# Efficient attention followed by a SwiGLU block: the order of the early loads, the last store and the written-out order of steps

## The chip, the cores and the metric

The kernel runs on one core of one Trainium2 chip. The metric is the device time of one execution in microseconds. A core has TensorE (PE, matmul; PEld is its weight load), VectorE (DVE), ScalarE (ACT), GpSimd (POOL) and SyncE (SP), which here only issues DMAs. Each engine works through its own queue in program order and waits on semaphores for the others.

## The reference

Eight batches of eight heads, 576 positions, head size 64. The attention has no score matrix: q is normalized by a softmax over the head dimension, k by a softmax over positions, and a 64 x 64 product of k and v is applied to q. A gated feed-forward block follows.

```python
q_s = softmax(q, axis=-1)                    # 8 x 8 x 576 x 64
k_s = softmax(k, axis=2)
kv = np.einsum('bhsd,bhse->bhde', k_s, v)
attn = np.einsum('bhsd,bhde->bhse', q_s, kv)
x = attn.transpose(0, 2, 1, 3).reshape(4608, 512)
g = x @ w_gate                               # 512 x 1536
out = (g * sigmoid(g) * (x @ w_val)) @ w_out # 1536 x 512, fp32 out
```

## The kernel before

**Attention, by batch b and group G.** A batch is loaded as six DMAs, q, k and v for each of two groups of four heads, 576 KB each, issued from SP (`load`, L89). The raw tiles of q and k have three buffers, those of v two. `exp` (eq, ek; L127) runs on ACT. `norm_sum` (ns; L143, L147) sums q's exponentials and takes reciprocals on DVE; `norm_mul` (nm with a DMA transpose, nd without; L152) scales them. `cast_v` (cv, L118 or L116) rounds v to bf16. `kv_pair` (kv) or `kv_kn` (kk) forms and normalizes the 64 x 64 products on PE (L192); `x_pair` (xx) or `x` (xz) multiplies q with them and writes the feed-forward input into the ring `xt`. In batches 0 and 1 q is transposed on PE (`tr`, L168), later by a DMA transpose issued from SP (`tr_dma`, L180).

**Feed-forward.** The tokens are taken in chunks: `chunk(-1)` holds batch 0's 576 tokens, chunk 0 the next 448, chunks 1 to 8 the rest, 512 tokens each; chunk 8 only finishes the output product. In chunk -1 the 12 blocks of 128 hidden columns are plain matmuls: `I` m computes the gate product and its Silu on ACT (L321), `J` m the value product and the multiplication on DVE (L324), into the ring `hr`. In later chunks some blocks are plain (`G`, `U`: L435), and the others are pairs `a` to `g` that use a seven-product (Strassen) scheme (L384); their weight sums `gt` come from `g_sum` (Q, T; L336) and their token sums `xs` from `x_sum` (X, Y). In the output product, `O` j s is half s of a plain 128-token unit (L473), of which chunk -1 has four; the letters `A` to `F` and `H` are the seven products of a 512-token `Quad` (L526), with sums `wt` (W) and `hs` (S) made on DVE. Results are copied to o_sb, of which there are five buffers, and stored with two DMAs of 64 rows for each 128 rows (`store`, L462).

**Weights.** `w_slice` (L104) and `wo_slice` (L112) load fp32 weights from HBM and round them to fp16 on the way; they are issued from GpSimd. wg and wv come in slices of 256, 256, 512 and 512 columns, wg and wv in turn, then w_out in three slices of four blocks (`wo`). The first waits for v(0,0) to land, and q of batch 1 waits for the first slice of w_out:

```python
load(1, 0, "q", q, after=w_dma[-3])
load(1, 1, "q", q)
for G in range(NG):
    load(1, G, "k", k)
    load(1, G, "v", v)
load_group(2, 0)
```

**Order.** The program order on every engine is the order of emission, and that is written out by hand: `PLAN_B` (chunk -1, with the attention of batch 1 and part of batch 2), `PLAN_0` (chunk 0), `PLAN` (chunks 1 to 5, with the attention of batch ci + 2 inside), `PLAN_N` (6 and 7), `PLAN_E` (8). A star moves a step to another engine: for Q, nd and xx from GpSimd or DVE as coded in `op`, for the products' copies from ACT to DVE, for e and g the multiplication from GpSimd to DVE, for H the copies from DVE to ACT. PSUM has eight banks in one pool; an I or J step takes two. ACT's exp and Silu need different tables, and each change between them puts an ACT_TABLE_LOAD into ACT's queue.

Of the kernel before, what the change touches and what calls it, by code (L numbers as in the profile page):

```python
# [16 lines left out]
def kernel(  # L17
# [19 lines left out]
    nc = tc.nc  # L37

    B, H, S, D = q.shape
# [58 lines left out]
    def w_slice(dst, src, c0, n):  # L98
        ap = bass.AP(
            tensor=src.tensor,  # L100
            offset=src[0, c0].offset,
            ap=[[d_ff, 128], [128 * d_ff, KT], [1, n]],
        )
        return nc.gpsimd.dma_start(out=dst[:, :, c0:c0 + n], in_=ap)  # L104

    def wo_slice(m0, n):
        ap = bass.AP(
            tensor=moe_w_out.tensor,
            offset=moe_w_out[m0 * 128, 0].offset,
            ap=[[d_model, 128], [128 * d_model, n], [1, d_model]],  # L110
        )
        return nc.gpsimd.dma_start(out=wo[:, m0:m0 + n, :], in_=ap)  # L112
# [187 lines left out]
    class First:  # L300
# [14 lines left out]

        def run(self, step, alt=False):
            if step == "I":
                self.sg = []
                for p_, (c, n) in zip(self.mm(wg, "g_ps"), self.parts):
                    self.sg.append(ff.tile([128, 512], FP32, tag="sg", name="sg"))  # L320
                    nc.scalar.activation(out=self.sg[-1][:, 0:n], in_=p_[:, 0:n], func=AF.Silu)  # L321
            else:
                for p_, sg, (c, n) in zip(self.mm(wv, "u_ps"), self.sg, self.parts):
                    nc.vector.tensor_mul(hr[:, self.m, c:c + n], sg[:, 0:n], p_[:, 0:n])  # L324

    def g_cols(w, kh, c0, c1):
        return w[:, 2 * kh:2 * kh + 2, :].rearrange("p k (j c) -> p k j c", j=2)[:, :, :, c0:c1]
# [22 lines left out]
            eng.tensor_sub(s[3], a12, s[1])  # L350

    def sg_tile():
        return ff.tile([128, 512], FP32, tag="sg", name="sg")

    class Pair:
        def __init__(self, c0, h, n, tsum, tc0):
# [147 lines left out]
    class Quad:  # L504
        def __init__(self, Q, kks, own=False):
            self.Q, self.r, self.kks = Q, (512 * Q) % RING, kks
            pool = (lambda n: ld.tile([128, 512], FP32, tag=n, name="os")) if own else None
            self.s_tile = (
                (lambda n: pool("q" if n == "s1" else "k")) if own
                else lambda n: sn.tile([128, 512], FP32, tag=n, name=n)  # L510
            )
            self.o_sb = [[None, None], [None, None]]

        def ot(self, t, p):
            if self.o_sb[t][p] is None:
# [42 lines left out]
        def run(self, step, alt=False):  # L558
            ceng = nc.vector if alt else nc.scalar
            two_f = lambda n: [f_tile(n) for _ in range(2)]  # L560
            if step == "A":
                self.x, self.s1 = two_f("ox"), self.two("s1")
                self.prod(self.x, self.raw_h(0, 0), self.raw_w(0, 0), True)
                self.copies(self.s1, self.x, ceng)
            elif step == "B":
                y = two_f("oy")
                self.prod(y, self.raw_h(1, 0), self.raw_w(1, 0), True)
                self.add(0, 0, y, self.s1)
            elif step == "C":
                self.w, self.s5 = two_f("ow"), self.two("s5")  # L570
                self.prod(self.w, self.sum_h(0), self.sum_w(0), True)
                self.copies(self.s5, self.w, ceng)
            elif step == "D":
                self.s2 = self.two("s2")
                self.prod(self.x, self.sum_h(1), self.sum_w(1), False)
                self.copies(self.s2, self.x, ceng)
            elif step == "F":
                self.prod(self.x, self.sum_h(2), self.sum_w(2), False)
                self.add(1, 1, self.x, self.s5)
            elif step == "E":  # L580
                self.prod(self.w, self.sum_h(3), self.raw_w(1, 1), False)
                self.add(0, 1, self.w, self.s2)
                self.store(0)
            elif step == "H":
                self.prod(self.x, self.raw_h(1, 1), self.sum_w(3), False)
                for p in range(2):
                    copy(
                        nc.scalar if alt else nc.vector,
                        self.ot(1, p)[:, 0:HN], self.x[p][:, 0:HN],
                    )  # L590
                    store(4 * self.Q + 2 + p, self.ot(1, p))

    make_identity(nc, ident)
    with tc.manual_schedule():
# [20 lines left out]
        cast_v(0, 0, nc.scalar)  # L615

        w_dma = []
        for c0, n in ((0, 256), (256, 256), (512, 512), (1024, 512)):
            w_dma.append(w_slice(wg, moe_w_gate, c0, n))
            w_dma.append(w_slice(wv, moe_w_val, c0, n))  # L620
        tc.add_manual_dep(w_dma[0].ins, dmas["v", 0, 0].ins.name, SYNC, reason="order of loads")
        for m0 in (0, 4, 8):
            w_dma.append(wo_slice(m0, 4))

        warm_up(WARM[0])
        for G in range(NG):
# [17 lines left out]
        x(0, 1, A)  # L644
        x(0, 1, Z)

        load(1, 0, "q", q, after=w_dma[-3])
        load(1, 1, "q", q)
        for G in range(NG):
            load(1, G, "k", k)  # L650
            load(1, G, "v", v)
        load_group(2, 0)

        n_ch = n_tok // 512 - 1

        def op(t, ci, c0, h, parts):
# [5 lines left out]
            if nm in ATT:  # L662
# [3 lines left out]
                if nm == "eq":  # L666
                    exp(b, G, "q")
                elif nm == "ek":
                    exp(b, G, "k")
                elif nm == "si":  # L670
                    nc.scalar.activation(out=warm, in_=warm, func=AF.Silu)
                elif nm == "cv":
                    cast_v(b, G, nc.vector if alt else nc.gpsimd)
                elif nm == "ns":
                    norm_sum(b, G)
                elif nm == "nm":
                    norm_mul(b, G, nc.vector if alt else nc.gpsimd)
                    tr_dma(b, G)
                elif nm == "lo":
                    if ci < 0:  # L680
                        load_group(b, 1)
                    else:
                        load_group(b + 1, 0)
                        load_group(b + 1, 1)
                elif nm == "kv":
                    kv_pair(b)
                elif nm == "xx":
                    x_pair(b, nc.scalar if alt else nc.vector)
                elif nm == "nd":
                    norm_mul(b, G, nc.gpsimd if alt else nc.vector)  # L690
                elif nm == "tr":
                    tr(1, G, BANKS[int(t[3])], nc.vector)
                elif nm == "kk":
# [48 lines left out]
        ORDER = (0, 1, 2, 3, 4, 5)  # L742
        gt2 = [None] * 4
        PLAN_B = """
        I0 J0 I1 I2 J1 J2 I3 J3 I4 I5 J4 J5 I6 I7 J6 I8 Q0* J7 J8 I9 I10 Q2* Q1* J9 eq0:1
        Q3 J10 eq1:1 I11 ns0:1 ns1:1 J11 ek0:1 ek1:1 nd1:1 O01 nd0:1* cv0:1 O11 O02* tr00
        cv1:1 O12 tr10 tr11 kk0:1 eq0:2 cv0:2 load:2 tr01 O21 xz00 kk1:1 xz01* ns0:2 O22
        nm0:2 ek0:2 xz10* O31 cv1:2 xz11 eq1:2 O32 ek1:2
"""
        PLAN_0 = """  # L750
        a0 b0 ns1 load v0 Y0 G4 a1 Y2 Y1* kv U4 c0 d0 G10 f0 b1 c1 Y3 nm1 W0 g0 d1 v1 a2
        e0 f1 e1 b2 c2 g1 d2 W1 v2 U10 a3 f2 G5 b3 g2 v3 e2 c3 d3* xx* e3 U5 f3 W2 X0 X2
        X1 G11 U11 g3* X3 W3
"""
        PLAN = """
        S002 G4 S022 S102 a0 b0 G10 d0 c0 A v0 a1 S042 eq0 S122 S142 S302 B S342 f0 S242
        b1 ek0 U4 S322 D S222 ek1 e0 eq1 cv0 S202 C* v1 cv1 g0 ns0 F E d1 H* a2 ns1 c1 f1
        silu nm0 b2 c2 nm1 e1 g1 d2* v2 a3 U10 f2 e2 load kv b3 g2 c3 d3 G5 v3 e3* f3 xx*
        X0 G11 U5 X1 U11 g3* X3 X2
"""  # L760
        PLAN_N = """
        a0 b0 c0 d0 A v0 T0* f0 S002 a1 b1 g0 d1 c1 S022 S102 S222 v1 e0 a2 S202 f1 e1 b2
        S042 c2 g1 d2 v2 S122 B f2 a3 T1 b3 c3 S242 S142 g2 e2 d3 S322 D v3 a4 f3 T2 C g3
        T3 d4 b4 e3 c4 v4 f4 S302 F a5 g4 b5 S342 d5 v5 e4 c5* f5 E X0 X1 e5* X3 X2* g5*
        H*
"""
        PLAN_E = """
        S202 S042 S022 S002 A S142 S122 S102 B C S322 S302 S342 D S222 S242 E F H*
"""
        chunk(-1, 0, S, PLAN_B)  # L770
        chunk(0, S, 1024 - S, PLAN_0)
# [33 lines left out]
```

The softmax here doesn't subtract the row's maximum and nothing guards it: scores larger than these inputs give would overflow.

## Time and profile before

| | us |
|---|---|
| median of 6 runs (lowest to highest) | 303.02 (302.1 to 306.46) |
| the profiled execution, its own time | 302.34 |
| its span in the trace | 300.3 |
| PE busy | 289.7 |
| DVE, ACT, POOL busy | 232.2, 210.7, 136.6 |
| chunk -1: first I to the end of the O steps | 15.57 to 57.6 |
| mean granted TensorE clock | 0.992 |

All times in the text are microseconds from the start of the span unless said otherwise. A line of a timeline has start, length, engine, line, operation, out<-in, shapes and count; in square brackets stands how long the engine sat idle before it and what released it. A row of waits has the sum, the number and the longest. Landing is the time from the start of a DMA's issue to its completion.

### The profile page before, as it was taken

The numbers are of one execution on the slowest core, as the hardware profiler recorded it, in microseconds if no ns is written. First come the engines' busy times: TensorE is split into PE (matmuls) and PEld (weight loads), VectorE is DVE, ScalarE is ACT, GpSimd is POOL, SyncE is SP. The second block draws the span as 40 slices with busy tenths as digits, with TensorE's granted clock in tenths as the row PEclk, the third lists the DMA queues.
The fourth block names the chain that finished last, engine by engine and source line by source line (L and its number), as shares of the span: only waits on it lengthen the run. The fifth ranks groups of instructions, "written<-read, shape, count | busy, mean of one in ns | idle before, by whom it ended". The sixth has DMA issues, their size and how long they took to land.

```text
span 300.3 us, 6895 instructions
## 1 busy us (share of the span) xinstructions
PE 289.7 (96%) x2644; PEld 227.8 (76%) x2644; DVE 232.2 (77%) x497; ACT 210.7 (70%) x385; POOL 136.6 (45%) x108
## 2 busy tenths in 40 slices
PE   8999979979999999999999999999999999999993
PEld 6777735568688758875887588758886888888882
DVE  2943956678898787888788878877888898895981
ACT  5754377687798579857995899479948776667530
POOL 1940165358309900890089008900794455275500
PEclk9999997999999999999999999999999999999999
DMA  7999999999003991289228931992180000600066
GB/s 268 273 182 206 236 395 310 293 268 314 0 3 68 175 389 62 62 168 368 99 52 174 357 111 40 194 387 75 43 180 0 2 0 4 139 2 0 3 139 140
DMA packets 38863, 46.43 MB, mean 155 GB/s; under 512 B 16304, under 2 KB 21936, under 8 KB 38832
## 3 DMA queue, kind: packets, MB, share of 16 engines
q1 hardware_dynamic: 33024, 41.30, 48.1%
q0 software_dynamic: 5808, 4.72, 10.2%
q8 instruction: 20, 0.33, 0.4%
q14 instruction: 11, 0.09, 0.1%
HBM read 37.75 MB, written 9.44 MB: 157 GB/s over the span
## 4 chain that ended last, share of the span: by engine, by line
PE 74%; DMA 16%; POOL 3%; SPq 2%; issue 1%; ACT 1%; DVE 1%; POOLq 0%; ACTq 0%; DVEq 0%
PE sx L384 19%; PE ox L526 14%; PE sw L384 10%; PE ow L526 7%; PE u_ps L435 7%; PE g_ps L435 6%; DMA wo<-in_moe_w_out_dram 5%; DMA v<-in_v_dram 5%; PE sy L384 5%; PE oy L526 3%; DMA qtd<-qs 3%; DMA q<-in_q_dram 2%; PE kv L192 2%; POOL vb L118 1%; POOL wg L104 1%
## 5 line engine op out<-in xcount | busy, mean ns | idle before, releaser
L418 POOL TENSOR_TENSOR hr<-sg,s 128x512 bf16<-128x512 f32 (+1 forms) x29 | 37.9, 1306 | 75.0 <-DVE s L417 74.0
L384 PEld LDWEIGHTS <-gt 128*128 128x128 f16 x576 | 56.2, 98 | 10.5 <-issue 0.7
L426 POOL TENSOR_TENSOR hr<-sg,s 128x512 bf16<-128x512 f32 (+1 forms) x28 | 35.6, 1270 | 35.4 <-ACT sg L425 35.4
L384 PE MATMUL sx<-xs,gt 128*128 128x256 f16 (+1 forms) x288 | 42.8, 271 | 0.0
L116 ACT COPY s<-sx 128x512 f32<-128x512 f32 (+1 forms) x66 | 38.2, 579 | 5.0 <-PE sx L384 4.2
L526 PEld LDWEIGHTS <-hs 128*128 128x128 bf16 x384 | 37.6, 98 | 5.4
L417 DVE TENSOR_TENSOR s<-sw,s 128x512 f32<-128x512 f32 (+1 forms) x36 | 24.5, 681 | 16.8 <-PE sw L384 16.5
L425 ACT ACTIVATE sg<-sx 128x512 f32<-128x512 f32 (+1 forms) x36 | 21.2, 590 | 19.9 <-PE sx L384 12.9
L152 POOL TENSOR_TENSOR qs<-eq,rr 128x1152 bf16<-128x1152 bf16 x14 | 29.5, 2120 | 11.4 <-DVE rr L147 11.4
L384 PEld LDWEIGHTS <-wg 128*128 128x128 f16 x288 | 27.7, 98 | 5.2
L421 DVE TENSOR_TENSOR s<-sx,s 128x512 f32<-128x512 f32 (+1 forms) x36 | 24.4, 679 | 8.9 <-ACT s L116 4.7
L526 PEld LDWEIGHTS <-hr 128*128 128x128 bf16 x288 | 28.2, 98 | 3.3
L143 DVE TENSOR_REDUCE rs<-eq 128x18 f32<-128x1152 bf16 x16 | 21.4, 1338 | 9.7 <-ACT eq L127 9.7
L410 ACT ACTIVATE sg<-s 128x512 f32<-128x512 f32 (+1 forms) x36 | 22.6, 626 | 8.0 <-DVE s L408 7.9
L116 ACT COPY s<-sw 128x512 f32<-128x512 f32 (+1 forms) x34 | 19.8, 583 | 8.9 <-PE sw L384 3.8
L408 DVE TENSOR_TENSOR s<-sy,s 128x512 f32<-128x512 f32 (+1 forms) x36 | 24.3, 674 | 1.4 <-ACT s L116 0.7
L435 PE MATMUL g_ps<-xt,wg 128*128 128x512 f16 (+1 forms) x96 | 24.3, 375 | 0.0
L526 PE MATMUL ox<-wt,hs 128*128 128x256 f16 x192 | 23.6, 273 | 0.0
L435 PE MATMUL u_ps<-xt,wv 128*128 128x512 f16 (+1 forms) x96 | 23.4, 375 | 0.0
L384 PE MATMUL sy<-xt,wg 128*128 128x256 f16 (+1 forms) x144 | 21.4, 271 | 0.0
L384 PE MATMUL sw<-xs,wv 128*128 128x256 f16 (+1 forms) x144 | 21.4, 271 | 0.0
L384 PE MATMUL sx<-xt,gt 128*128 128x256 f16 (+1 forms) x144 | 21.4, 271 | 0.0
(99 smaller groups left out, 570.8 us busy)
## 6 DMA issues: line engine op xcount, KB each, us to landing
q<-in_q_dram SPq DMA_DIRECT2D x16, 576.0 KB, 6.7
k<-in_k_dram SPq DMA_DIRECT2D x16, 576.0 KB, 8.4
v<-in_v_dram SPq DMA_DIRECT2D x16, 576.0 KB, 8.8
out_dram<-o_sb SPq DMA_DIRECT2D x72, 128.0 KB, 2.4
wo<-in_moe_w_out_dram POOLq DMA_DIRECT2D x3, 512.0 KB, 18.2
wg<-in_moe_w_gate_dram POOLq DMA_DIRECT2D x2, 512.0 KB, 11.1
wv<-in_moe_w_val_dram POOLq DMA_DIRECT2D x2, 512.0 KB, 12.7
wg<-in_moe_w_gate_dram POOLq DMA_DIRECT2D x2, 256.0 KB, 5.7
```

The costliest lines, as they stand in the source:

```text
L116: nc.scalar.copy(out=out, in_=in_)
L143: nc.vector.reduce_sum(out=rs, in_=s["eq"].rearrange("p t h d -> p (t h) d"), axis=mybir.AxisListType.X)
L152: eng.tensor_mul(s["qs"].rearrange("p t (h d) -> p (t h) d", d=64), s["eq"].rearrange("p t h d -> p (t h) d"), s["rr"].to_broadcast([128, ...
L384: nc.tensor.matmul(out=bank[:, h * j:h * j + h], lhsT=wgt(kk, j), rhs=rhs[:, kk, 0:h], start=first and j == 0 and kk == 0, stop=kk == 1, s ...
L408: nc.vector.tensor_add(self.s1, self.y[:, 0:w], self.s1)
L410: nc.scalar.activation(out=self.sa[:, 0:w], in_=self.s1, func=AF.Silu)
L417: nc.vector.tensor_add(self.s2, self.w[:, 0:w], self.s2)
L418: meng.tensor_mul(self.out(0), self.halves(self.sa), self.halves(self.s2))
L421: nc.vector.tensor_add(self.s5, self.x[:, 0:w], self.s5)
L426: meng.tensor_mul(self.out(1), self.halves(sb), self.halves(self.s5))
L435: nc.tensor.matmul(out=ps[:, 0:self.n], lhsT=w[:, kk, 128 * self.m:128 * self.m + 128], rhs=xt[:, kk, self.r:self.r + self.n], start=(kk = ...
L526: nc.tensor.matmul(out=dst[p][:, 0:HN], lhsT=lhs(kk, p), rhs=rhs(kk), start=start and i == 0, stop=i == HM - 1, skip_group_check=True,)
```

## The change

- Weights: wv's first two slices become one of 512 columns, and both first slices of wg go ahead of it. `w_dma` then has wg 0, wg 256, wv 0, wg 512, wv 512, wg 1024, wv 1024, w_out 0, 4, 8, numbered from 0. The first slice of w_out waits on GpSimd for wg 1024 to land.
- Loads: q of batch 1 waits for wv 512. k and v of batch 1 wait for w_out 4, w_out 8 and one another; batch 2's loads wait each for an earlier load of the chain. The load of v(2,1) alone stays at the plan's `load`.
- The Silu results of an I step share one tile of 576 columns in place of two of 512; the buffers stay four.
- In the last Quad, the second half of each of H's stores is issued from ACT.
- All five plans have a new order, and some stars change: in `PLAN_B` Q0 and nd1 move to GpSimd; in `PLAN` a2's copy moves to DVE, C's copies to ACT and e3's multiplication to GpSimd; in `PLAN_E` D's copies move to DVE.

```diff
-                self.sg = []
-                for p_, (c, n) in zip(self.mm(wg, "g_ps"), self.parts):
-                    self.sg.append(ff.tile([128, 512], FP32, tag="sg", name="sg"))
-                    nc.scalar.activation(out=self.sg[-1][:, 0:n], in_=p_[:, 0:n], func=AF.Silu)
+                ps = self.mm(wg, "g_ps")
+                self.sg = ff.tile([128, S], FP32, tag="sg", name="sg")
+                for p_, (c, n) in zip(ps, self.parts):
+                    nc.scalar.activation(
+                        out=self.sg[:, c:c + n], in_=p_[:, 0:n], func=AF.Silu
+                    )
...
-                    store(4 * self.Q + 2 + p, self.ot(1, p))
+                    engs = (nc.sync, nc.scalar) if self.last else (nc.sync, nc.sync)
+                    store(4 * self.Q + 2 + p, self.ot(1, p), engs=engs)
...
-        for c0, n in ((0, 256), (256, 256), (512, 512), (1024, 512)):
-            w_dma.append(w_slice(wg, moe_w_gate, c0, n))
-            w_dma.append(w_slice(wv, moe_w_val, c0, n))
+        w_dma.append(w_slice(wg, moe_w_gate, 0, 256))
+        w_dma.append(w_slice(wg, moe_w_gate, 256, 256))
+        w_dma.append(w_slice(wv, moe_w_val, 0, 512))
+        for c0 in (512, 1024):
+            w_dma.append(w_slice(wg, moe_w_gate, c0, 512))
+            w_dma.append(w_slice(wv, moe_w_val, c0, 512))
         tc.add_manual_dep(w_dma[0].ins, dmas["v", 0, 0].ins.name, SYNC, reason="order of loads")
+        load(1, 0, "q", q, after=w_dma[4])
+        load(1, 1, "q", q)
         for m0 in (0, 4, 8):
             w_dma.append(wo_slice(m0, 4))
+        tc.add_manual_dep(w_dma[7].ins, w_dma[5].ins.name, SYNC, reason="order of loads")
...
-        load(1, 0, "q", q, after=w_dma[-3])
-        load(1, 1, "q", q)
-        for G in range(NG):
-            load(1, G, "k", k)
-            load(1, G, "v", v)
-        load_group(2, 0)
+        load(1, 0, "k", k, after=w_dma[8])
+        load(1, 0, "v", v)
+        load(1, 1, "k", k, after=w_dma[9])
+        load(1, 1, "v", v, after=dmas["k", 1, 0])
+        load(2, 0, "q", q, after=dmas["v", 1, 0])
+        load(2, 0, "k", k, after=dmas["k", 1, 1])
+        load(2, 0, "v", v, after=dmas["v", 1, 1])
+        load(2, 1, "q", q, after=dmas["q", 2, 0])
+        load(2, 1, "k", k)
...
-        I0 J0 I1 I2 J1 J2 I3 J3 I4 I5 J4 J5 I6 I7 J6 I8 Q0* J7 J8 I9 I10 Q2* Q1* J9 eq0:1
-        Q3 J10 eq1:1 I11 ns0:1 ns1:1 J11 ek0:1 ek1:1 nd1:1 O01 nd0:1* cv0:1 O11 O02* tr00
-        cv1:1 O12 tr10 tr11 kk0:1 eq0:2 cv0:2 load:2 tr01 O21 xz00 kk1:1 xz01* ns0:2 O22
-        nm0:2 ek0:2 xz10* O31 cv1:2 xz11 eq1:2 O32 ek1:2
+        I0 I1 I2 I3 J0 J1 J2 I4 Q0 I5 I6 J3 I7 J4 eq0:1 J5 J6 eq1:1 J7 ns1:1 I8 I9 ns0:1
+        I10 nd1:1* nd0:1* I11 J8 J9 J10 J11 ek0:1 Q1* O01 tr00 Q2* O11 ek1:1 cv0:1 tr01
+        cv1:1 load:2 O02 kk0:1 O21 tr10 xz01* xz00* Q3 O12 tr11 eq0:2 kk1:1 O31 ns0:2
+        nm0:2 ek0:2 xz10* cv0:2 O22 eq1:2 cv1:2 ek1:2 xz11 O32*
...
-        a0 b0 ns1 load v0 Y0 G4 a1 Y2 Y1* kv U4 c0 d0 G10 f0 b1 c1 Y3 nm1 W0 g0 d1 v1 a2
-        e0 f1 e1 b2 c2 g1 d2 W1 v2 U10 a3 f2 G5 b3 g2 v3 e2 c3 d3* xx* e3 U5 f3 W2 X0 X2
-        X1 G11 U11 g3* X3 W3
+        a0* ns1 b0 G4 v0 G10 Y0 Y1* U4 kv G5 Y2* d0 U10 c0 nm1 a1 f0 b1 c1 g0 d1 v1 Y3 a2
+        W0 e0 f1 U5 b2 c2 g1 d2 v2 W1 e1 e2 f2 xx* a3* W2 b3 c3 g2 d3* G11 v3 f3 e3 U11 X0
+        load g3* X1 X2 W3 X3
...
-        S002 G4 S022 S102 a0 b0 G10 d0 c0 A v0 a1 S042 eq0 S122 S142 S302 B S342 f0 S242
-        b1 ek0 U4 S322 D S222 ek1 e0 eq1 cv0 S202 C* v1 cv1 g0 ns0 F E d1 H* a2 ns1 c1 f1
-        silu nm0 b2 c2 nm1 e1 g1 d2* v2 a3 U10 f2 e2 load kv b3 g2 c3 d3 G5 v3 e3* f3 xx*
-        X0 G11 U5 X1 U11 g3* X3 X2
+        G4 a0 ek0 S242 b0 S002 S202 U4 A S102 d0 eq0 S042 c0 eq1 B S302 S142 v0 S022 G10
+        S122 f0 S342 a1 S222 e0 b1 U10 D g0 C cv0 v1 d1 S322 c1 ns0 a2* F nm0 f1 E ek1 b2
+        cv1 v2 ns1 nm1 c2 g1 H* d2* a3 e1 f2 kv g2 b3 c3 d3 load e2 G5 v3 e3 f3 xx* U5
+        silu X0 X2 G11 X1 g3* U11 X3
...
-        S202 S042 S022 S002 A S142 S122 S102 B C S322 S302 S342 D S222 S242 E F H*
+        S002 S022 S102 S122 S042 S142 S302 S342 A S242 S322 B S202 S222 C D* E F H*
```

More of the change, by code (lines that the diff above doesn't have):

```diff
@@ L317, in run @@
             if step == "I":
-                self.sg = []
-                for p_, (c, n) in zip(self.mm(wg, "g_ps"), self.parts):
-                    self.sg.append(ff.tile([128, 512], FP32, tag="sg", name="sg"))
-                    nc.scalar.activation(out=self.sg[-1][:, 0:n], in_=p_[:, 0:n], func=AF.Silu)
-            else:
-                for p_, sg, (c, n) in zip(self.mm(wv, "u_ps"), self.sg, self.parts):
-                    nc.vector.tensor_mul(hr[:, self.m, c:c + n], sg[:, 0:n], p_[:, 0:n])
+                ps = self.mm(wg, "g_ps")
[4 more added lines that the diff above has]
+                    )
+            else:
+                for p_, (c, n) in zip(self.mm(wv, "u_ps"), self.parts):
+                    nc.vector.tensor_mul(
+                        hr[:, self.m, c:c + n], self.sg[:, c:c + n], p_[:, 0:n]
+                    )
     def g_cols(w, kh, c0, c1):
@@ L352, in sg_tile @@
     def sg_tile():
-        return ff.tile([128, 512], FP32, tag="sg", name="sg")
+        return ff.tile([128, S], FP32, tag="sg", name="sg")
     class Pair:
@@ L512, in __init__ @@
             self.o_sb = [[None, None], [None, None]]
+            self.last = Q == n_tok // 512 - 1
         def ot(self, t, p):
@@ L680, in op @@
                     if ci < 0:
-                        load_group(b, 1)
+                        load(b, 1, "v", v)
                     else:
@@ L760 @@
+        cv1 v2 ns1 nm1 c2 g1 H* d2* a3 e1 f2 kv g2 b3 c3 d3 load e2 G5 v3 e3 f3 xx* U5
+        silu X0 X2 G11 X1 g3* U11 X3
 """
         PLAN_N = """
[L762 to L765, printed above, removed]
+        a0 S022 S002 b0 A T0 d0 c0 v0 a1 f0 b1 S042 c1 T1* e0 g0 d1 v1 B f1 S122 a2 b2
@@ L766 @@
+        S102 g1 d2 v2 c2 e1 a3 S222 f2 C g2 S242 b3 S202 S142 d3 v3 e2* c3 f3 a4 D T2 g3
+        T3 b4 d4 v4 e3 c4 S342 f4 a5 F g4 d5 b5 S302 c5 S322 X0* v5 e4 f5 E e5* X1 X3* g5*
+        X2 H*
 """
         PLAN_E = """
-        S202 S042 S022 S002 A S142 S122 S102 B C S322 S302 S342 D S222 S242 E F H*
+        S002 S022 S102 S122 S042 S142 S302 S342 A S242 S322 B S202 S222 C D* E F H*
 """
```

## Prediction

> **What bounds the kernel now.** I read the page first, then busy time by stage, then the waits and the timeline where a stage has a hole.
>
> ```profile
> PE 289.7 (96%) x2644; PEld 227.8 (76%) x2644; DVE 232.2 (77%) x497; ACT 210.7 (70%) x385; POOL 136.6 (45%) x108
> ```
>
> TensorE is busy 96%, so 10.6 us of holes are all that a better order can win. The stages (length, then PE, PEld, DVE, ACT, POOL busy, then the granted clock) say where they lie:
>
> ```profile
> 15.57:39.11 23.54, 23.54 (x196) 18.69 (x193) 13.34 (x30) 9.81 (x25) 5.67 (x6) 1.00 1.23 224
> 39.11:45.40 6.29, 3.94 (x20) 1.67 (x18) 3.50 (x6) 6.07 (x7) 3.42 (x2) 1.00 1.05 393
> 45.40:57.60 12.20, 12.15 (x101) 6.01 (x102) 8.69 (x21) 7.53 (x11) 6.65 (x5) 0.86 0.93 306
> 57.60:62.10 4.50, 2.76 (x37) 2.11 (x37) 2.76 (x4) 4.38 (x5) 1.44 (x2) 1.00 1.11 221
> 82.40:284.50 202.10, 202.09 (x1871) 163.57 (x1869) 169.08 (x360) 154.14 (x282) 99.26 (x73) 1.00 0.43 117
> 295.20:300.30 5.10, 0.00 (x0) 0.00 (x0) 0.00 (x0) 0.37 (x1) 0.00 (x0) 0.86 0.64 137
> ```
>
> The 24 I and J steps (15.57 to 39.11) and everything from 82.4 to 284.5 have no hole: there the new order can only lose. The winnable time is 2.35 us at 43, 1.74 us at 60, a stretch at 0.86 clock, and the tail. The waits name the first two:
>
> ```profile
> PE o_ps L473 <- DVE hr L324: 2.4, 1, 2.4
> PE kv L192 <- POOL vb L118: 1.7, 1, 1.7
> ```
>
> The timeline shows what stood behind the first:
>
> ```profile
> 36.21 4.58 POOL L336 TENSOR_TENSOR gt<-wg,gt 128x1024 f16<-128x1024 f16 x2 [17.11 <-DVE gt L336]
> 39.27 1.28 ACT L127 ACT_TABLE_LOAD   x1 [3.18 <-DMA q<-in_q_dram]
> 40.57 2.22 ACT L127 ACTIVATE eq<-q 128x1152 bf16<-128x1152 f32 x2
> 42.80 1.28 ACT L321 ACT_TABLE_LOAD   x1
> 44.10 0.71 ACT L321 ACTIVATE sg<-g_ps 128x320 f32<-128x320 f32 x2
> 45.40 0.39 PE L473 MATMUL o_ps<-wo,hr 128*128 128x512 f16 x1 [2.35 <-DVE hr L324]
> ```
>
> ScalarE sat until q of batch 1 landed (39.2), did both exps, reloaded its table, and only then I11's Silu; J11's product and the output matmul queued behind it. The hole was followed by one 3.4 us window at half clock (46.0 to 49.4: 0.55), which cost 1.7 us. The second hole waits for v(2,1), issued only at 52.2 because SP had first waited for cast v(1,0) and issued four stores; it landed at 60.8.
>
> **DMA arrivals.** From the issue rows of short windows (issue plus time to landing): weight slices landed at 15.0, 16.3, 18.1, 19.4, 22.1, 24.7, 27.8 and 29.9, wo at 32.4, 35.0 and 39.0. From 16 to 36 us the weights move at 205 GB/s as written in 16 bits, about 2.6 us for each 512-column slice. A q, k or v load at about 400 GB/s takes 1.5 us. q(1,0), issued at 32.4, landed at 39.2, then at about 1.5 us spacing q(1,1) 40.6, k(1,0) 42.1, v(1,0) 44.1, k(1,1) 45.6, v(1,1) 47.1.
>
> **The change, part by part.**
>
> *First weights.* wv 0:512 becomes the third slice. J0 now stands at 15.57 + 4 x 0.98 = 19.5 and needs it; the same bytes had landed by 19.4. I4 at 22.4 needs wg 512, 22.1 before. Cost 0, at most 0.5. Joining two sg tiles into one lets four I steps run ahead in four buffers and adds no instruction.
>
> *q of batch 1.* It now waits for wv 512:1024 (24.7), with two slices queued in front. Before, q was issued with two slices in front too, and landed 6.8 and about 8 us after issue: 31.5 and 33. eq0 and eq1 are emitted between I7 and I8. ACT: eq1 ends 34.2, table load to 35.5, I8's first Silu (0.44) 35.9. J8 stands at 15.57 + 20 x 0.98 = 35.2 and reuses I8's two PSUM banks (eight banks, two for each step), so it waits **0.9 us** (0 if q comes 1 us earlier). DVE: both norm_sums (1.6 each) end 37.4, J8 to J11's products follow to 40.9, and only O02 needs the last of them.
>
> Here the trace and a rule differ. In the 1 us window from 34, two us after q was issued, and in that from 36:
>
> ```profile
> q0 software_dynamic: 207, 0.21, 125.3%
> ```
> ```profile
> q1 hardware_dynamic: 115, 0.26, 73.4%
> q0 software_dynamic: 67, 0.06, 34.9%
> ```
>
> Not one packet of q moved until the weights were nearly through. The Trainium skill ("DMA: Bandwidth & Descriptors", Queues, rings and completion order) says that each DMA engine goes round-robin between queues with work, a packet at a time. By the rule q shares with the two slices in front, 2.1 MB plus 1.2 MB at 0.41 MB/us from about 26: q(1,1) lands near 33, the sum above. Read literally, the row says that q waits until GpSimd's queue is empty; since wo is now queued behind wg 1024 at about 28, that is 40.6 again (the slow rival). First come, first served fits the row and gives 33; I take 33.
>
> *wo chained behind wg 1024.* GpSimd waits there from about 15.5 to 28; behind it stand only Q0 (needs wv 1024, about 31.4) and nd, so nothing is held. The two q loads push wo back 3 us: 35.4, 38.0, 40.6. O01 at about 40 needs the second, O02 at 43 the third: free.
>
> *Q0 and nd1 move from DVE to GpSimd.* Q0 takes 4.6 us there (row at 36.21; 1.3 on DVE): 31.4 to 36.0; two norm_muls of 2.12 each end at 40.2; tr00 wants the first qs at 41.4. Free, but the cover is 1 us.
>
> *k and v of batch 1, batch 2.* They start behind wo. All bytes ahead of k(1,0) are those of before, so k(1,0) cannot come before 42.1; with 0.5 us for the wait on landings, k 42.6 and v 44.6. Cast of v(1,0) on GpSimd 1.15 (2.2 beside DVE): 45.8. PE: J11 ends 40.0, O01, tr00, O11, tr01, O02 (1.31 each, tr 0.3) reach 44.5, so kk0 waits **1.3 us** (0 to 2.4). Afterwards nothing is late: cast v(1,1) by 49.9, kk1 at 51. The O and transpose part took 18.5 us of which 2.4 was wait and 1.7 slow clock; 0.2 more goes with small gaps, so it needs 14.2 and would end at 53.3; with both waits **55.5 against 57.6: 2.1 us won**. Each load waits on one two places ahead, three in flight, each 3.7 us at the start of the kernel (0.74 to 4.4) against 1.5 of transfer: just enough to keep 1.5 us spacing. v(2,1) lands at about 56.7 instead of 60.8. The stores of O0 queue behind these loads on SP; their o_sb has five buffers for four units, so nobody waits.
>
> *Chunk 0.* kv stands 3.1 us into it, at 58.6. GpSimd: cast v(1,1) 49.9, Q3 54.5, norm_mul 56.6, the two casts 59.0. Its second half wants that at 59.2. I leave 0.3: **1.4 us won** of 1.7. load of batch 3 now comes behind the second transpose on SP instead of ahead of it, so the transpose (9.5 us to landing before) no longer queues behind six loads; GpSimd gives its qs at 63.3, x_pair stands near 69.
>
> *Steady chunks.* A chunk is 30.3 us of PE. ACT's calls now alternate: ek0, then eq0 eq1, then ek1 with Silu between, four table loads for two. The skill ("ScalarE: Activation LUTs", Table sets: the hidden batching unit) says to batch calls by set. Taken as a cost on the path, 2 x 1.283 us (the row) in five chunks is 12.8 us and the kernel ends near 312. But the chunk from 112.6 has ACT busy 23.9 of 30.3; with 2.6 more it is 26.5. Walking ACT's queue with the row durations, it falls 4 us behind PE at G10 (Silu at 10.7 for a matmul ended at 7.0) and is level again at a3. a1's copy is done at 11.2, wanted by d1 at 12.6; d1's copy at 14.0, wanted at 15.3. So hidden. The tightest place is on DVE: H's copies and d2's copy behind norm_sum end at 21.1, f2 wants it at 20.9. I charge **0.4 us** in all (0 to 4). The last chunk: D's copies move to DVE and end near 292.0, F wants them at 292.35: free.
>
> *Last store.* SP issued the four at 294.94 to 297.37, 0.59 each. With half on ACT the second pair waits only for its copy, delayed 0.3 by ACT's issue, and ends at 296.6: **0.7 us** (0 to 0.8).
>
> **Sum.** 2.1 + 1.4 + 0.7 - 0.4 = 3.8 us. The profiled execution took 302.34 (span 300.3): 298.5. The median shown is 303.02, 0.7 above it: **299.2**.
>
> **Rivals.**
> - *q starved* (slower). q waits for GpSimd's whole queue: q(1,1) at 40.6, J8 at 43.5 instead of 35.2. Then 17.8 us of PE work, 0.6 of wait and 1.7 at half clock: the O part ends at 63.7, +6.1; less 2.1 elsewhere, 306.3, as median **307.0**. It decides from q(1,1) landing at about 38, where the gain is gone. For: the window at 34. Against: the rule, and at 10 to 11 us GpSimd's first slice did not push the earlier loads aside.
> - *Half clock again.* The wait at kk0 grows over 2 us and a window at half clock follows, as at 46: **300.9**. Against: the 1.7 us wait at 60 brought none.
> - *Steady chunks stall* 0.5 us each, seven of them: **302.3**. For: 26.5 of 30.3 on ACT, f2's negative margin. Against: 202.1 us without a hole with a plan of the same density.
> - *Neither wait arises* (q and v land 1 to 1.5 us earlier): **297.0**.
>
> **Chances.** Forecast 0.46, starved 0.14, half clock 0.12, stalls 0.16, no waits 0.12. A measurement here tells about 1%, so faster means under 300.0: 0.39 of the forecast, the no-wait case and a little of half clock, 0.54. Slower (over 306.0): most of starved and the worst of the stalls, 0.15. Between: 0.31. The range 296.6 to 304.5 holds all but starved and the ends.
>
> **What would show it.** Right: eq's exp at 31 to 34; J8 waiting under 1.5 us on an I8 Silu; kv of batch 1 waiting 1 to 2 us for a GpSimd cast; no half-clock window; no wait at kv of batch 2; 24 to 26.5 us of ACT in a steady chunk with PE full; first matmul of chunk 0 near 55.5; last store issued at 296.6 less the gain ahead. Wrong: exp of q(1,1) after 38, or PE under 30 us in a 30.3 us chunk.

## The result and the profile after

The changed kernel took **301.16 us** in the median of 21 runs (300.0 to 305.46), beside 302.71 for the kernel before: ratio **0.9931, interval 0.9908 to 0.9955**, about 2.1 us faster; the medians lie 1.6 us apart. The ratio is one of means, and it leaves out one execution of the kernel before and two of the changed one that ran in a slower state. The forecast was 299.2, a gain of 3.8. The profiled execution took 299.87 us with a span of 298.0 (before: 302.34 and 300.3).

On the page, the row of busy engines shows that GpSimd and ScalarE took over work, as meant, and that TensorE's busy time is almost what it was (289.0 against 289.7):

```profile
PE 289.0 (97%) x2644; PEld 227.5 (76%) x2644; DVE 230.3 (77%) x485; ACT 219.4 (74%) x399; POOL 145.9 (49%) x115
```

TensorE's waits after (sum, number, longest):

```profile
PE kv L192 <- POOL vb L118: 1.7, 2, 1.1
PE warm_ps L256 <- DVE zero L610: 1.1, 1, 1.1
PE u_ps L310 <- ACT sg L321: 1.0, 1, 1.0
PE sx L388 <- DVE s L118: 0.4, 1, 0.4
```

The 2.4 us wait of w_out's product is gone. In its place stands a wait of 1.0 at J8 (`u_ps`) and one at K^T V of batch 1. The wait at K^T V of batch 2, which should have gone, is there at 1.1; the two `kv` waits share the first row.

Busy time by stage after, in the stages used before, the second row joining two of them (length, then PE, PEld, DVE, ACT, POOL, granted clock, DMA share, GB/s):

```profile
16.04:40.85 24.81, 23.84 (x196) 18.68 (x193) 12.66 (x28) 16.06 (x32) 10.28 (x7) 1.00 1.17 227
40.85:55.66 14.81, 14.20 (x122) 7.06 (x120) 9.59 (x24) 7.74 (x12) 8.61 (x6) 1.00 0.96 312
55.66:60.60 4.94, 3.86 (x41) 2.45 (x41) 4.20 (x6) 3.91 (x4) 2.57 (x3) 1.00 1.21 318
79.80:282.60 202.80, 202.80 (x1875) 163.84 (x1873) 168.49 (x351) 164.61 (x300) 104.02 (x77) 1.00 0.44 117
292.80:298.00 5.20, 0.38 (x4) 0.10 (x1) 0.00 (x0) 0.51 (x2) 0.00 (x0) 0.92 0.59 148
```

Four things are to be seen. The granted clock is 1.00 in the second row, where it was 0.86 in most of that stage. The DMA rate in that row is 312 GB/s, although this stage lives on loads. The steady row is full, with ScalarE at 164.6 us where it had 154.1 in a stretch of nearly the same length. The last row still has 5.2 us in which hardly anything but stores runs.

The chunk -1 stage in the timeline, ScalarE and TensorE around q of batch 1:

```profile
31.59 1.28 ACT L127 ACT_TABLE_LOAD   x1 [2.86 <-DMA q<-in_q_dram]
32.88 2.22 ACT L127 ACTIVATE eq<-q 128x1152 bf16<-128x1152 f32 x2
35.11 1.28 ACT L321 ACT_TABLE_LOAD   x1
36.41 2.53 ACT L321 ACTIVATE sg<-g_ps 128x320 f32<-128x320 f32 x8
36.90 4.22 PE L310 MATMUL u_ps<-xt,wv 128*128 128x320 f16 x32 [0.97 <-ACT sg L321]
```

The exps run at 33 to 35, not 40 to 43, and J8 waits 0.97 us for I8's first Silu behind the second table load. And the two casts that K^T V waited for, of v(1,0) and v(2,1):

```profile
44.92 1.14 POOL L118 CAST vb<-v 128x1152 bf16<-128x1152 f32 x1 [3.70 <-DMA v<-in_v_dram]
59.37 1.15 POOL L118 CAST vb<-v 128x1152 bf16<-128x1152 f32 x1 [2.29 <-DMA v<-in_v_dram]
60.57 0.65 PE L192 MATMUL kv<-vb,ek 64*128 64x129 bf16 x16 [1.08 <-POOL vb L118]
```

GpSimd sat idle 3.70 and 2.29 us until the two landed, v(2,1) at 59.3: it was the transfers that were late, not the engine.

Span by part, from the two timelines. H+A stands for the product H of one Quad and A of the next, which run back to back; the last H+A opens the last Quad:

| part | before | after | measured | forecast |
|---|---|---|---|---|
| start to the first I | 15.57 | 16.04 | +0.47 | 0 |
| first I to chunk 0's first matmul | 42.04 | 39.62 | -2.4 | -2.1 |
| chunk 0 | 21.3 | 21.0 | -0.3 | -1.4 |
| chunks 1 to the last H+A | 205.7 | 206.0 | +0.2 | +0.4 |
| last H+A to the end | 15.65 | 15.38 | -0.3 | -0.7 |
| span | 300.3 | 298.0 | -2.3 | -3.8 |

The first row belongs to nothing that was edited: the first I started between 15.6 and 16.3 us in the kernels below, whatever they changed.

### The profile page after: what moved, and what is told of

It is laid out like the page before. It is cut to its first block, busy times and chain, and to the rows that moved or that the text cites. A ratio compares the mean times of both kernels' runs of the same rounds, so it can differ in the third digit from the quotient of the medians.

```text
span 298.0 us, 6915 instructions
## 1 busy us (share of the span) xinstructions
PE 289.0 (97%) x2644; PEld 227.5 (76%) x2644; DVE 230.3 (77%) x485; ACT 219.4 (74%) x399; POOL 145.9 (49%) x115
## 4 chain that ended last, share of the span: by engine, by line
PE 77%; DMA 13%; POOL 3%; ACT 2%; DVE 2%; issue 1%; ACTq 0%; SPq 0%; POOLq 0%
PE sx L388 21%; PE ox L531 13%; PE sw L388 10%; PE ow L531 7%; PE u_ps L439 7%; PE g_ps L439 6%; PE sy L388 5%; DMA v<-in_v_dram 5%; DMA wv<-in_moe_w_val_dram 4%; PE oy L531 4%; DMA q<-in_q_dram 3%; PE kv L192 2%; PE o_ps L477 1%; ACT eq L127 1%; DVE rs L143 1%
## 5 line engine op out<-in xcount | busy, mean ns | idle before, releaser
L422 POOL TENSOR_TENSOR hr<-sg,s 128x512 bf16<-128x512 f32 (+1 forms) x32 | 40.5, 1266 | 69.0 <-DVE s L421 68.6
L430 POOL TENSOR_TENSOR hr<-sg,s 128x512 bf16<-128x512 f32 (+1 forms) x28 | 35.7, 1275 | 18.9 <-ACT sg L429 18.4
L152 POOL TENSOR_TENSOR qs<-eq,rr 128x1152 bf16<-128x1152 bf16 x15 | 31.8, 2123 | 18.4 <-issue 10.7
L116 ACT COPY s<-sx 128x512 f32<-128x512 f32 (+1 forms) x59 | 34.5, 584 | 4.9 <-PE sx L388 4.6
L429 ACT ACTIVATE sg<-sx 128x512 f32<-128x512 f32 (+1 forms) x36 | 22.0, 610 | 13.7 <-PE sx L388 12.7
L116 ACT COPY s<-sw 128x512 f32<-128x512 f32 (+1 forms) x36 | 21.0, 582 | 4.6 <-PE sw L388 3.2
L439 PE MATMUL u_ps<-xt,wv 128*128 128x512 f16 (+1 forms) x96 | 24.3, 375 | 0.0
L127 ACT ACTIVATE ek<-k 128x1152 bf16<-128x1152 f32 x16 | 18.6, 1163 | 6.8 <-DMA k<-in_k_dram 6.6
L531 PE MATMUL ox<-wt,hs 128*128 128x256 f16 x192 | 23.6, 273 | 0.0
L127 ACT ACTIVATE eq<-q 128x1152 bf16<-128x1152 f32 x16 | 18.8, 1179 | 4.0 <-DMA q<-in_q_dram 4.0
```

Of the source, the lines that this page charges most:

```text
L116: nc.scalar.copy(out=out, in_=in_)
L127: nc.scalar.activation(out=s["e" + what], in_=raw[what, b, G].rearrange("p h (t d) -> p t h d", d=64), func=AF.Exp,)
L152: eng.tensor_mul(s["qs"].rearrange("p t (h d) -> p (t h) d", d=64), s["eq"].rearrange("p t h d -> p (t h) d"), s["rr"].to_broadcast([128, ...
L422: meng.tensor_mul(self.out(0), self.halves(self.sa), self.halves(self.s2))
L430: meng.tensor_mul(self.out(1), self.halves(sb), self.halves(self.s5))
L439: nc.tensor.matmul(out=ps[:, 0:self.n], lhsT=w[:, kk, 128 * self.m:128 * self.m + 128], rhs=xt[:, kk, self.r:self.r + self.n], start=(kk = ...
```

## Experiments

Times are medians; each ratio, of means, is to the kernel before on the same chip, with its interval. Spans and rows are of the profiled execution. `w_dma` lists the weight loads in order of issue.

### The two halves alone: the loads without the order, and the reverse

First the early loads of the change, w_out's chain among them, in the kernel before, with its old order of steps:

```diff
+        load(1, 0, "q", q, after=w_dma[5])
+        load(1, 1, "q", q)
...
-        load_group(2, 0)
+        load(1, 0, "k", k, after=w_dma[9])
...
-                        load_group(b, 1)
+                        load(b, 1, "v", v)
```

> The plans, the weight slices, the Silu tiles and the stores of before; only the loads of batches 1 and 2 are chained as in the change. Theory (the gain comes from q landing 7 us earlier, not from the new order): q(1,1) lands near 33, so in the old place of eq0 and eq1, behind I10, ScalarE finds them there; I11's Silu ends near 41.6 instead of 44.8, the 2.35 us hole at 43 and the half-clock window behind it go, and the O part ends near 54.5 to 55.5 instead of 57.6. kv of batch 2 then waits for v(2,1) at about 60.5 as in the changed kernel. Span 298 to 298.8. Rival (the new order is what closes the hole; an early q is of no use where eq is emitted late): the hole stays over 1.5 us, span 299.5 or more.

Measured: 305.09, ratio 1.006 (1.0022 to 1.0097), span 303.3. Slower than before. The span lies in the rival's range, but not for the rival's reason: the hole at the O steps is gone, and a larger one opens:

```profile
PE kv L192 <- POOL vb L118: 6.9, 3, 5.1
```

v(2,1) is issued in the old order's place of `load:2`, behind four stores of O0 on SP, at 56.02 us, and K^T V of batch 2 waits 5.1 us for its cast. A stretch at half clock follows (0.57 from 63.5 to 67.5).

The reverse, the changed kernel with the loads of before, its weight slices too:

```diff
-        load(1, 0, "q", q, after=w_dma[4])
-        load(1, 1, "q", q)
...
+        load(1, 0, "q", q, after=w_dma[-3])
+        load(1, 1, "q", q)
```

> All of the change but the loads, which are those of before (q of batch 1 lands near 40.6). Theory: the new order has eq0 and eq1 in front of I8's Silu, so J8 waits on ScalarE until about 43.5 (over 7 us), a half-clock window follows, and the kernel is slower than before: span 303 to 306. Rival (the order is what brings the gain): span below 300.

Measured: 309.92, ratio 1.0217 (1.0131 to 1.0303), span 308.0. The theory held in kind, and the size was above it. The new order puts both exps of q(1,·) ahead of I8's Silu, so all of q's lateness now falls on TensorE:

```profile
45.09 6.53 PE L310 MATMUL u_ps<-xt,wv 128*128 128x320 f16 x32 [9.26 <-ACT sg L321]
```

Those 32 matmuls took 6.53 us instead of 4.22, because TensorE ran at half clock after the wait (0.50 from 40 to 50 us). Each half, cut like this, costs time; only the two together gain.

Was it only the place of v(2,1)'s load that spoiled the first? The same kernel with `load:2` ahead of O02:

```diff
-  ... O01 nd0:1* cv0:1 O11 O02* tr00
-  cv1:1 O12 tr10 tr11 kk0:1 eq0:2 cv0:2 load:2 tr01 ...
+  ... O01 nd0:1* cv0:1 O11 cv1:1 load:2 O02* tr00
+  O12 tr10 tr11 kk0:1 eq0:2 cv0:2 tr01 ...
```

> The run with the loads alone, and load:2 (the load of v(2,1)) emitted ahead of O02 and its stores instead of behind them. There v(2,1) was issued at 56.0, after four stores on SP, and kv of batch 2 waited 5.1 us. Theory (that place on SP's queue, not the order of TensorE's steps, is what the loads alone lacked): v(2,1) is issued near 52, kv waits under 1.5 us, no half-clock window follows, span 299 to 300. Rival: kv of batch 2 still waits over 3 us, because the old order needs something else later too, span over 301.5.

Measured: 304.4, ratio 1.0017 (0.9975 to 1.0058), span 301.9: no different from before. The 5.1 us wait fell to 1.13, as expected, but others show (two rows of waits, then two of the timeline):

```profile
PE kv L192 <- POOL vb L118: 3.3, 3, 1.8
PE xa L273 <- DMA qtd<-qs: 2.2, 1, 2.2
```
```profile
50.60 0.70 PE L192 MATMUL kv<-vb,ek 64*128 64x129 bf16 x18 [1.76 <-POOL vb L118]
76.68 0.33 PE L273 MATMUL xa<-qtd,kn 64*64 64x320 bf16 x4 [2.23 <-DMA qtd<-qs]
```

The wait of 1.76 us at K^T V of batch 1 was followed by a stretch at half clock (0.52 from 51.5 to 55.0), which the theory had excluded. The wait for the transpose is new. In the old PLAN_0 the loads of batch 3 stand ahead of the second transpose on SP, and x_pair now reaches that transpose before it has landed. So the trace points to at least two places on SP's queue where the new order is needed: v(2,1) ahead of O0's stores, which this run tested, and the transpose ahead of batch 3, which no run tested by itself.

### The chain of k and v loads

All manual waits of the loads of batches 1 and 2 taken away, except that of k(1,0) on a slice of w_out:

```diff
-        load(1, 1, "k", k, after=w_dma[9])
-        load(1, 1, "v", v, after=dmas["k", 1, 0])
-        load(2, 0, "q", q, after=dmas["v", 1, 0])
...
+        load(1, 1, "k", k)
+        load(1, 1, "v", v)
+        load(2, 0, "q", q)
```

> The changed kernel, but behind k(1,0) no load of batches 1 and 2 waits for another load; their order is the same. Landing theory: between 43 and 55 us the chained loads moved about 300 GB/s, the unchained ones of before 391; without the chain the loads land 1.5 us apart again, v(2,1) near 57 instead of 59.3, kv of batch 2 waits no longer (1.08 us in the changed kernel), span 1.0 to 1.5 us lower. Rival (the chain protects the first arrivals): with six loads in flight k(1,0) and v(1,0) share the DMA engines with those behind, land later, kk's wait grows by 1 us or more and the span does not fall.

Measured: 299.76, ratio 0.9887 (0.9819 to 0.9956), span 299.3. TensorE no longer waits for a GpSimd cast of v; the largest cast wait left is 0.5 us, on a DVE cast. From chunk 0's first matmul to the first A product it took 22.3 us against 23.6 in the changed kernel. This execution lost that again at J8, with a wait of 2.26 us and a stretch at half clock after it. With four executions its interval overlaps the changed kernel's, so the whole time does not yet tell the two apart.

And with k(1,0) waiting for w_out's first slice instead of its second (`after=w_dma[7]`):

> The unchained version with one edit more: k of batch 1 waits for the first slice of w_out instead of the second, so that no bubble stands between the last weights and k(1,0) (in the changed kernel the DMA rate fell to 53 to 147 GB/s for 1 us near 39). Landing theory: k(1,0) and v(1,0) land about 1 us earlier, and so do all loads behind them; the first kk of batch 1 does not wait for its cast. Gain over the unchained version 0 to 1 us, since J8's wait for q is the same: median 299 to 300. Rival (the last slice of w_out is pushed back by the loads and O02, which needs it, waits for it): no gain, or 1 us lost.

Measured: **298.8, ratio 0.9835 (0.9791 to 0.9879)**, span 296.8, the fastest of all. The same kernel once more, on another occasion:

> The same kernel as the one in which only k(1,0) still waits for another load (for the first half of w_out), run again beside the two that follow so that the three share a chip. It measured 298.8 us, ratio 0.9835, span 296.8. Expected again: ratio 0.981 to 0.988 to the kernel before. If its lead over the changed kernel (0.9931) was luck of the chip, the ratio comes out near 0.99 or above.

Measured: 298.86, ratio 0.9857 (0.981 to 0.9905). The medians agree, and both lie some 2 us below the changed kernel's. The profiles of the changed kernel and of the first of these two runs show 1.2 us of that (spans 298.0 and 296.8), all of it between chunk 0's first matmul and the first A product, where the wait at K^T V of batch 2 is gone; the rest was not traced. Behind that wait stand the DMA rates. The changed kernel from 43 to 55 us, GB/s in 40 slices and the sum:

```profile
GB/s 353 392 415 399 269 207 177 307 307 369 392 246 215 230 238 300 261 323 307 207 238 315 315 330 376 399 392 384 422 353 277 253 253 304 200 230 284 292 307 361
DMA packets 1681, 3.66 MB, mean 305 GB/s; under 512 B 95, under 2 KB 95, under 8 KB 1680
```

The kernel before, whose k and v loads are not chained, from 37 to 48:

```profile
DMA packets 1998, 4.32 MB, mean 393 GB/s; under 512 B 120, under 2 KB 141, under 8 KB 1996
```

And the first unchained one from 41 to 55:

```profile
DMA packets 2428, 5.29 MB, mean 378 GB/s; under 512 B 134, under 2 KB 145, under 8 KB 2427
```

At its start this window still holds the first packets of k(1,0); from 43 to 55, as above, the mean is 393. With mostly three loads issued and not yet landed, as in the chain, the rate sinks to some 200 to 250 GB/s again and again. The dips are what the chain costs: nine loads of 0.59 MB at 305 instead of 390 GB/s take 17.4 us instead of 13.6.

### Where q of batch 1 stands

q one slice of the weights earlier:

```diff
-        load(1, 0, "q", q, after=w_dma[4])
+        load(1, 0, "q", q, after=w_dma[3])
```

> The changed kernel with one edit: q of batch 1 waits for wg 512 instead of wv 512, about 2.5 us earlier. Landing theory: J8's wait of 0.97 us goes, but kk of batch 1 cannot start before v(1,0) has landed and been cast (46.1 in the changed kernel), so its wait grows from 0.6 to about 1.6 and the span stays within 0.3 us. Rival (the forecast's own sum, where each wait counts by itself): the span falls by 0.9 to 1.0 us.

Measured: 301.4, ratio 0.994 (0.9898 to 0.9983): no gain over the change. q was issued 1.8 us earlier (22.87) and ScalarE's table load came only 0.5 earlier, so this says little about whether waits add up.

w_out not chained behind wg 1024, which tells readings of q's late packets apart:

```diff
-        tc.add_manual_dep(w_dma[7].ins, w_dma[5].ins.name, SYNC, reason="order of loads")
```

> The changed kernel without the wait of w_out's first slice for wg 1024, so that when q of batch 1 is issued at about 25 five weight slices instead of two stand queued ahead of it. Order theory (what is queued on the engines first is moved first): q(1,1) lands 5 us later or more, 38 to 41, J8 waits 6 us or more, a half-clock window follows, span 303 or more. Rival (the DMA engines go round the queues, so the length of the other queue does not matter): q(1,1) lands within 1.5 us of 33 to 35 and J8 waits under 3 us.

Measured in one run: 300.11, span 298.3. w_out was now issued at 15 to 17 us, ahead of q. From 30 to 32 us (packets, MB, share of the 16 engines; q1 carries q, q0 the weights and w_out):

```profile
q1 hardware_dynamic: 189, 0.40, 58.3%
q0 software_dynamic: 187, 0.19, 55.6%
```

Packet for packet the two queues share evenly, although all of w_out had been queued before q. That is the round-robin rule of the prediction, once q moves, and it refutes first come, first served. q(1,1) landed at 35.0 and J8 waited 2.40:

```profile
38.04 2.15 PE L310 MATMUL u_ps<-xt,wv 128*128 128x320 f16 x15 [2.40 <-ACT sg L321]
```

So in these two profiles w_out's chain is worth about 1.4 us at J8. q still moved nothing at first. In the changed kernel, with q issued at 24.64, the 1 us windows from 27 and from 28 show (one row, then two):

```profile
q0 software_dynamic: 203, 0.21, 126.2%
```
```profile
q1 hardware_dynamic: 121, 0.28, 72.7%
q0 software_dynamic: 73, 0.06, 38.4%
```

About 3.4 us passed before q's first packet, the same with w_out queued or not.

Next, can J8's wait be removed by putting q ahead of the weights of group 1024, on top of the fastest kernel?

```diff
-        load(1, 0, "q", q, after=w_dma[4])
+        load(1, 0, "q", q, after=w_dma[3])
...
+        tc.add_manual_dep(w_dma[5].ins, w_dma[3].ins.name, SYNC, reason="order of loads")
```

> The unchained kernel with q of batch 1 moved ahead of the weights of group 1024 (it waits for the weights of group 512, and those of 1024 wait for the same). Theory (the next landing decides): q(1,1) lands near 29 to 30 us instead of 33, the wait of 1.47 us at J8 goes, but K^T V of batch 1 still waits for the cast of v(1,0) near 46 us, so its wait of 0.3 grows to about 1.5; the span stays within 0.4 us of 296.8. Rival (waits add up): the 1.2 to 1.5 us are gained, and the span is 295.3 to 295.6.

Measured: 302.36, ratio 0.9976 (0.9943 to 1.0009), span 300.0. Both theories fell. J8's wait is gone, and four others came:

```profile
PE o_ps L477 <- DMA wo<-in_moe_w_out_dram: 1.7, 1, 1.7
PE tp L168 <- POOL qs L152: 1.3, 1, 1.3
PE kv L192 <- POOL vb L118: 1.2, 1, 1.2
...
PE g_ps L310 <- DMA wg<-in_moe_w_gate_dram: 0.5, 1, 0.5
```

The DMA rates from 30 to 40 us show one reason. Around 32 to 34 us, and again at 36.5, the engines ran nearly dry: w_out waited for a landing, was issued at 31.69, and the rate was back at 200 only 3 us later:

```profile
GB/s 205 213 213 209 201 209 197 197 107 45 21 12 16 29 94 78 131 188 197 201 188 201 209 209 209 176 86 74 107 119 119 160 197 180 233 205 201 193 209 201
```

With K^T V emitted later, so that O21 fills its wait:

```diff
- cv1:1 load:2 O02 kk0:1 O21 tr10 ...
+ cv1:1 load:2 O02 O21 tr10 kk0:1 ...
```

> As the kernel with q first, and K^T V of batch 1 emitted after O21 and the first transpose of batch 1 instead of before O21. Theory: if K^T V's own landing was the next wait, O21 now fills it and the span comes out 1.0 to 1.6 us below the unchained kernel's, about 295.5, the median about 297.5. Rival: a later load (v(1,1), or v(2,1) for batch 2) takes the wait's place, and nothing is gained: span 296.4 to 297.2.

Measured: 301.17, ratio 0.9924 (0.9889 to 0.9958), span 299.2: neither theory's span. K^T V waits no more, w_out and the first transpose do (1.4 and 1.7 us). Last, the same without w_out's chain, which closes the hole in the DMA rates:

> As the kernel with q first and K^T V late, but w_out no longer waits for the weights of group 1024, so it stands queued when they run out. Theory (the chains let the DMA engines run dry, 50 GB/s at 32 to 34 us and 131 at 36 to 38, and that made w_out late): the hole closes, the waits for w_out (1.4 us) go, k(1,0) is issued near 35 instead of 37.4, and the span falls by 1 to 2.5 us from 299.2, to 296.7 to 298.2; the wait at the first transpose for qs (1.7, behind Q0 on GpSimd, which needs the last weights) stays. Rival (it is q's 1.2 MB ahead of the weights that makes all the rest late, not the holes): w_out still lands near 45 and the span stays at 298.8 or above.

Measured: 299.74, ratio 0.9891 (0.986 to 0.9923); the profiled execution, with a span of 299.8, has a stretch at half clock behind its wait at the first transpose, while eight of the eleven have spans of 297.1 to 298.5, seven of them in the theory's range. The hole is closed (203 GB/s from 30 to 40 us) and the waits for w_out are gone, so the drained engines had been the reason for those. k(1,0) came only 0.4 us earlier (36.96). The longest wait left is the one that was expected to stay:

```profile
PE tp L168 <- POOL qs L152: 2.2, 1, 2.2
```

and GpSimd's timeline says why:

```profile
34.36 4.20 POOL L340 TENSOR_TENSOR gt<-wv,wg 128x1024 f16<-128x1024 f16 x2 [8.09 <-DMA wv<-in_moe_w_val_dram]
```

With q in front, wv 1024 lands 2.6 us later than in the fastest kernel (where this row starts at 31.72). Q0 starts later, both qs behind it on GpSimd are later, and the first transpose waits. J8's wait has been exchanged for one of the same size, and nothing is won over 298.8.

### The last store

All stores on SP, the rest as changed:

```diff
-                    engs = (nc.sync, nc.scalar) if self.last else (nc.sync, nc.sync)
+                    engs = (nc.sync, nc.sync)
```

> The changed kernel with the last store on SP alone, as before. Theory (the last eight stores drain at about 0.62 us each however they are issued): the time from the last Quad's first matmul to the end of the span is 0.2 to 0.4 us longer than the changed kernel's 15.4. Rival (the forecast: issue on SP is the limit): 0.7 us longer or more.

Measured: 300.74, ratio 0.9899 (0.9865 to 0.9932), span 298.6; from the last H+A to the end 15.64 us, with two queues 15.38. The issues end at 295.69 in this kernel,

```profile
290.65 5.04 SPq L466 DMA_DIRECT2D out_dram<-o_sb  x8
```

and at 294.5 in the changed one:

```profile
292.96 0.56 ACTq L466 DMA_DIRECT2D out_dram<-o_sb  x1
...
294.02 0.50 ACTq L466 DMA_DIRECT2D out_dram<-o_sb  x1
```

So the last issue ends 1.2 us earlier, 0.8 counted from the last H+A, and the tail only 0.26, as the theory had it: the drain of the data sets its end, not the issues. That is one profile of each kernel; the whole times (300.74 and 301.16) can't tell this step from none.

## Why the prediction was half right

**First weights, and wo chained behind wg 1024: right.** No I or J step before J8 waited. Taking wo's chain away moved q(1,1) from about 33 to 35.

**q of batch 1: the landings right, J8's wait in part by luck.** Predicted: q landing at 31.5 and 33, J8 waiting 0.9. Measured: the table load that waited for q starts at 31.59, J8 waits 0.97. Two slips cancel in that wait. eq1 was put to end at 34.2, but both exps stand behind the table load, and the rows that the prediction shows (1.28 and 2.22 us) give 35.0; it ended at 35.10. J8 for its part stood ready at 35.9, not at 35.2, 0.47 of it because the first I came later. With the first slip alone the wait would have been about 1.5. The landings were the delays of before carried over; the sum by the rule (3.3 MB at 0.41 MB/us from 26) gives 34, not 33.

Of the three readings weighed there, the Trainium skill's rule that each DMA engine takes turns between its queues, a packet at a time ("DMA: Bandwidth & Descriptors", Queues, rings and completion order), is what the run without wo's chain shows once q moves (189 and 187 packets). First come, first served, which I had allowed to fit, is refuted, and q was not starved as in the literal reading. All three lacked one thing: the 3.4 us before q's first packet.

**k and v of batch 1: right in sum.** Predicted a wait of 1.3 at K^T V and chunk 0 at 55.5; measured 0.61 and 55.66. The J steps ended 0.85 later than reckoned (40.85, not 40.0), and K^T V waited that much less, because the landing of v(1,0) was nearly as forecast (44.9, not 44.6) and released it at about the same time. No half-clock stretch followed in the profiled execution.

**Each load waits on one two places ahead: the step that failed.** I took 3.7 us from issue to landing, from the kernel's start, and 1.5 us of transfer, so that three in flight would "just" keep the spacing. In the chain, a load took 5.1 to 6.1 us (v(1,1) 5.1, q(2,0) 5.3, k(2,0) 6.1); three in flight of that length give 1.7 to 2.0 us each. From k(1,0) at 43.1 to v(2,1) at 59.3, nine intervals took 16.2 us, 1.8 each instead of 1.5. v(2,1) was forecast for 56.7 and landed at 59.3, 2.6 us late, of which v(1,0) had brought 0.3. The 3.7 had come from the first load of the kernel, which began on idle engines. Time to landing alone is not what counts: in the first unchained kernel it is longer still (medians of 7.7 to 8.9 us), but with more loads in flight the engines move 393 GB/s instead of 305.

**Chunk 0: mis-sized by that.** Forecast 1.4 us won, measured 0.3; the missing 1.1 is the wait of 1.08 at K^T V of batch 2. Without the chain this wait is gone, and the stretch from chunk 0 to the first A takes 22.3 to 22.4 us in the three profiles of the two unchained kernels, against 23.2 to 23.6 in the four that keep the change's chain and order (the change, q earlier, w_out free, one queue). This is shown, not only argued.

**Steady chunks: right.** Forecast 0.4 us lost, measured 0.2. The four table loads in place of two sit beside a full TensorE: 202.80 of 202.80 us busy, ScalarE at 164.6. To batch calls by table set, as the Trainium skill advises ("ScalarE: Activation LUTs", Table sets: the hidden batching unit), could have bought nothing in this stretch, as the prediction's row of ScalarE had said.

**Last store: mis-sized.** Forecast 0.7, measured 0.3. I counted issue time alone, and that fell as forecast (by 0.8 us, counted from the last H+A). The stores' data goes on after the last issue, and in the two profiles the tail between that issue and the end grew, from 2.9 us before (297.37 to 300.3) to 3.5 (294.5 to 298.0). The issue had hidden part of the drain.

**What is not in the sum.** The profiled execution is 1.4 above its forecast of 298.5, its span 1.5 above: 0.5 at the first I, 1.1 in chunk 0 and 0.4 in the tail, less 0.5 in the O part and the steady chunks that went better. The median lies 1.3 above that execution, where I had allowed 0.7. Together that is the 2.0 us between 299.2 and 301.2.

**What stays open.** Why q's first packet takes 3.4 us was not separated into causes. Nor was an order found in which neither J8 nor the first transpose waits.

## What to carry to other kernels

A chain of loads must be sized with the time to landing under load (5 to 6 us here), not the one of an idle queue, and where no order of landing needs it, leaving the loads unchained on one queue is simpler; here, with k(1,0) issued one slice earlier, it was also some 2 us faster. When loads and the order of the work are changed together, neither may work alone: the loads by themselves cost 0.6% (nothing that could be measured with v(2,1) moved ahead), the order by itself 2.2%, and the pair gained 0.7%. A transfer moved to the front is paid for by those behind it, so before moving it, follow each of those to its first user, on GpSimd's queue as well as on TensorE's.

## What the runs showed of the hardware

**The first packets come late beside a full queue.** q's load, issued at 24.64 with weight slices in flight on GpSimd's queue, moved its first packet at about 28. In the kernel with q first it was issued at 22.39, when those slices were nearly through, and moved packets from the window at 23 to 24 on. Whether the weights still queued are what holds q back was not tested by itself.

**Half clock after a single wait.** Waits of TensorE of 2.2 to 2.35 us were followed by some 3.4 us at half clock in four kernels (before, the first unchained, the repeated one and the last with q first), one of 5.11 (the loads alone) by as much, and one of 9.26 by 10 us that took in part of the wait. The length of the wait does not settle it: one of 1.76, with v(2,1) moved ahead, was followed by such a stretch, while one of 2.23 in the same profile, one of 2.40 without wo's chain, and those of 1.66 to 1.74 in four kernels were not. The repeated unchained kernel, from 38 to 44 us (clock in the third column from the end):

```profile
38.00:40.00 2.00, 1.78 (x11) 1.20 (x11) 1.97 (x5) 2.00 (x8) 1.66 (x1) 0.82 1.23 218
40.00:42.00 2.00, 2.00 (x10) 1.19 (x9) 0.95 (x4) 1.55 (x2) 2.00 (x2) 0.50 1.04 378
42.00:44.00 2.00, 2.00 (x15) 1.47 (x14) 1.04 (x3) 0.28 (x1) 0.54 (x1) 0.83 1.04 399
```

This costs about 1.7 us, and J8's wait lies near these lengths: 1.5 to 2.3 us in the three profiles of the two unchained kernels. It would explain much of the spread between executions of one kernel. Of the repeated kernel's six, four took 298.3 to 299.0 us at a mean granted clock of 0.997 to 1.000, and two took 300.7 and 301.1 at 0.992 and 0.994; 3.4 us at half clock are 0.006 of such a span. The stretch itself was seen only in the profiled execution, the one of 301.1, and the link was not tested by itself.
